# Attention and two feed-forward networks: weights converted in pairs in place, casts on ScalarE, split products with v from the second batch on

## The chip, the cores and the metric

The kernel runs on one core of one Trainium2 chip. The metric is the device time of one execution in microseconds (us); of several executions the median counts. The profile is of one execution, and its durations and waits are read from the hardware's own records.

## The reference

Three parts follow one another; all inputs and the output are float32.

```python
def _attn_ref(q, k, v, f):            # q, k, v: (4, 8, 576, 64), f: (4, 8, 576)
    scores = scale * np.matmul(q, k.transpose(0, 1, 3, 2))
    log_f = np.log(np.clip(f, 0.0001, 1.0))
    cum = np.cumsum(log_f, axis=-1)
    decay = cum[:, :, :, None] - cum[:, :, None, :]
    scores = np.where(causal, -1000000000.0, scores + decay)
    attn = np.exp(scores - np.max(scores, axis=-1, keepdims=True))
    attn = attn / (np.sum(attn, axis=-1, keepdims=True) + 1e-09)
    return np.matmul(attn, v).astype(np.float32)

def _moe_ref(x, w_gate, w_val, w_out):   # x: (2304, 512), d_ff 1536; these weights are
    g = x @ w_gate                       # float64
    silu = g * (1.0 / (1.0 + np.exp(-g)))
    return (silu * (x @ w_val) @ w_out).astype(np.float32)

def _moe2_ref(x, w_gate, w1, w2):        # 8 experts, inner width 1024
    P = balance(x @ w_gate)              # exp, then 8 rounds of row and column scaling
    return sum(P[:, e:e + 1] * (np.maximum(x @ w1[e], 0.0) @ w2[e]) for e in range(8))
```

(The last function's body is put in short words.) The weights of the first network arrive as 64-bit words, which the kernel turns into float32 itself.

## The kernel before

**Precision.** TensorE multiplies in a fast format of float32 (float32r in the code). To keep float32's accuracy, an operand is split in two float32r values, a high part (a cast, `hi`) and the rest (`rest`, line 153: source minus high part, on GpSimd unless told otherwise). A product is then the sum of three fast products (`three`, line 157), or of two where one operand is treated so. Products with plain float32 operands are also possible on TensorE; each shows as two matmul records.

**Attention** (`attn_unit`, line 233) works batch by batch, head by head, two heads to a pair. `load` (257) fetches q and k of a head twice, into both halves of the partitions, and the row of decays; line 277 casts q and k to float32r on VectorE, and two `rest` calls on GpSimd make their low parts. `scores` (286) multiplies a block of 128 queries with the keys, adds the decay and takes the minimum on VectorE (line 304), and the exponential on ScalarE (line 308). `trans` (331) transposes the probabilities on TensorE and copies them from PSUM. `pv` (351) multiplies them with v in two ranges of queries. `recips` (312) adds 1e-9 to the sums of a pair of heads (line 315, VectorE), takes the reciprocal, transposes it, and sends it through DRAM to be broadcast; `fold` (376) multiplies it in.

In the first two batches (`first`, `b < FRONT`, FRONT = 2) the products with v are plain float32: `trans` copies (line 343, on VectorE for blocks 2 and 4, on ScalarE for the others), into one set of buffers for each head of a pair; `pv` makes one product a block and one copy (365). In the last two batches the products are split: v is cast on ScalarE (250, 253) and its rest made on GpSimd (252, 254), with both parts side by side in one stationary operand; `trans` casts (347, ScalarE) and subtracts (348, VectorE) into one set of buffers, `pv` makes two products a block, and line 373 copies and 374 adds the two halves. `spaces` (205) allocates these buffers. Batches 0 and 1 also take their PSUM for scores from the pool of the first network, which does not run yet.

**The first network** (`moe_unit`, line 415) goes through d_ff in six slices of 256. A slice needs six pieces of weights: gate and value for each of two blocks of 128 columns, and two output pieces. `convert` (107) makes a piece from float64: a load of 512 KB to `st` (four issues for gate and value, one for an output piece), on VectorE the exponent's bits (123), on ScalarE their shift (125), on VectorE sign and exponent (126), the exponent alone (128) and the mantissa's product (129), on GpSimd a sum (131), then the high part (134, ScalarE) and the rest (135, GpSimd; its time is under line 155). The result goes to a ring of eight buffers (`wring`) and is also stored in DRAM (`wsplit`, 136). Each of the 36 pieces is converted once, during batches 0 and 1 of this network; batches 2 and 3 fetch the stored pieces (`fetch`, 148).

**The second network** starts behind it and is most of the time: lines 605 to 672, with weights prefetched.

**Order.** `merge` (21) interleaves steps of attention and of the network by their costs: batch 0 alone, batch 1 with the first six conversions, batch 2 with the network on batches 0 and 1 (converting on the way), batch 3 with the network on batch 2, then the network on batch 3 with the preparation of the second network (510 to 558). The compiler's scheduler then orders each engine's queue by its own model of times, so loads can be issued far ahead of their place in the program; each engine works its queue in order. All transfers are issued by SP. The loads of the first PACE (4) pieces are held behind the last load of q and k issued before them.

Of the kernel before, what the change touches and what calls it, by code (L numbers as in the profile page):

```python
# [8 lines left out]
F32 = mybir.dt.float32  # L9
F32R = mybir.dt.float32r  # L10
# [23 lines left out]
def attention_two_ffns(ctx: ExitStack, tc: tile.TileContext, qkT, vt, f, w_gate, w_val, w_out, g2, w1, w2, out):  # L34
# [3 lines left out]
    DFF = w_gate.shape[1]  # L38
# [16 lines left out]
    wring = m_ctx.enter_context(pool("wring", 8))  # L55
# [36 lines left out]
    bases = const.tile([P, 2], F32, name="bases")  # L92
    nc.vector.memset(bases[:, 0:1], -8.0 * (896 << 4))
    nc.vector.memset(bases[:, 1:2], -8.0 * (897 << 4))
    wpieces = []
    for s in range(nsl):
        for c in range(2):
            f0 = s * FS + c * P
            for w in (w_gate, w_val):
                wpieces.append((w[:, f0:f0 + P].rearrange("(k p) f -> p k f", p=P), KD, bases[:, 0:1]))  # L100
        for c in range(2):
            f0 = s * FS + c * P

            wpieces.append((w_out[f0:f0 + P, :], 1, bases[:, 1:2]))
    wsplit = [dram.tile([P, 2, HP], F32, name=f"wsplit{i}") for i in range(len(wpieces))]

    def convert(i):
        src, nk, base = wpieces[i]
        st = cvp.tile([P, 4 * HP + 4], U16, tag="st", name="st", bufs=2)
        n = HP // nk  # L110
        with tc.issue_after(last_qk[0].ins) if i < PACE else ExitStack():
            if nk == 1:
                nc.sync.dma_start(out=st[:, 1:1 + 4 * HP], in_=src.bitcast(U16))
            else:
                for k in range(nk):
                    nc.sync.dma_start(out=st[:, 1 + 4 * n * k:1 + 4 * n * (k + 1)], in_=src[:, k, :].bitcast(U16))
        mid = st.bitcast(U32)[:, 0:2 * HP].rearrange("p (i t) -> p i t", t=2)[:, :, 1]
        top = st[:, 4:4 + 4 * HP].rearrange("p (i t) -> p i t", t=4)[:, :, 0]
        y = cvp.tile([P, HP], U16, tag="y", name="y")
        z = cvp.tile([P, HP], U16, tag="z", name="z")  # L120
        g = cvp.tile([P, HP], U16, tag="g", name="g")
        v = cvp.tile([P, HP], F32, tag="v", name="v")
        nc.vector.tensor_scalar(out=y, in0=top, scalar1=0x7fff, scalar2=None, op0=ALU.bitwise_and)

        nc.scalar.activation(out=z, in_=y, func=AF.Relu, scale=8.0, bias=base)
        nc.vector.scalar_tensor_tensor(
            out=g, in0=top, scalar=0x8000, in1=z, op0=ALU.bitwise_and, op1=ALU.bitwise_or)
# [3 lines left out]
        nc.gpsimd.tensor_tensor(out=v, in0=v, in1=g.bitcast(BF16), op=ALU.add)  # L131
        t = wring.tile([P, 2, HP], F32R, tag="w", name="w")
        hi, lo = t[:, 0], t[:, 1]
        nc.scalar.copy(out=hi, in_=v)
        rest(lo, v, hi)
# [6 lines left out]
    PACE = 4  # L142

    FRONT = 2
    VIA = 2
    ONV = (2, 4)

    def fetch(i):
        t = wring.tile([P, 2, HP], F32R, tag="w", name="w")
        last_dma[0] = nc.sync.dma_start(out=t.bitcast(F32), in_=wsplit[i])  # L150
        return t
# [53 lines left out]
    def spaces(b):  # L205


        first = b < FRONT
# [24 lines left out]
    def attn_unit(b):  # L233
        first = b < FRONT
        pairs, heads = {}, {}

        def load_pair(hp):
            if hp == 0:
                if b != VIA:
                    room(b)  # L240
                if b in (0, FRONT):
                    spaces(b)
# [14 lines left out]
        def load(h):  # L257
# [19 lines left out]
            nc.vector.tensor_copy(out=qkh, in_=qk)  # L277
# [8 lines left out]
        def scores(h, qi):  # L286
# [9 lines left out]
            for n, (c0, w, use) in enumerate(chunks):  # L296
                ps = (ps_m if first else ps_s).tile([P, 512], F32, tag="m" if first else "s", name="ps_s")
# [14 lines left out]
        def recips(hp):  # L312

            rc = small.tile([P, 10], F32, tag="rc", name="rc", bufs=2)
            nc.vector.tensor_scalar_add(out=rc, in0=sms[hp % 2], scalar1=1e-9)
# [15 lines left out]
        def trans(h, qi):  # L331
            pt = heads[h][-1].pop(qi)
            alt = first and qi % 3 == 2
# [78 lines left out]
    def group(w):  # L412
        return [w[0], w[2]], [w[1], w[3]], w[4:6]
# [348 lines left out]
```

## Time and profile before

| What | Value |
|---|---|
| Median of three runs | 2308.84 us |
| Lowest and highest | 2297.91 and 2312.47 us |
| The profiled execution | 2307.45 us |
| Its span, first to last instruction | 2305.7 us |
| Mean granted TensorE clock | 0.990 of full speed |
| TensorE matmul busy | 2246.2 us (97%) |
| TensorE weight loads busy | 2037.2 us (88%) |
| VectorE busy | 1724.4 us (75%) |
| GpSimd busy | 867.1 us (38%) |
| ScalarE busy | 809.5 us (35%) |

The engines are named PE (TensorE; PEld its weight loads), DVE (VectorE), ACT (ScalarE), POOL (GpSimd) and SP (SyncE, which issues the transfers; SPq is its sequencer). Busy times of matmuls overlap their waits, so weight loads tell better how full TensorE is. A row of a group gives line, engine, operation, output and inputs, shapes and count, then busy time, mean ns of one, and the idle time before them with what ended it. An execution is 1.75 us longer than its span.

### The profile page before, as it was taken

How to read it: one execution, taken by the hardware profiler on the slowest of the kernel's cores; microseconds unless marked ns; L12 is line 12 of the kernel's file. 1: busy time of each engine (PE TensorE's matmuls, PEld its weight loads, DVE VectorE, ACT ScalarE, POOL GpSimd, SP SyncE). 2: the span in 40 equal slices, each digit the busy share in tenths (PEclk: the TensorE clock that was granted, in tenths of full speed). 3: DMA queues.
4: the chain of work that ended last, by engine and by line, in shares of the span. 5: the costliest groups of instructions: out<-in, count | busy, mean ns of one | idle time of the engine just before them, and what ended most of it. 6: DMA issues, size and time to landing. Idle time of an engine off the chain costs nothing.

```text
span 2305.7 us, 36555 instructions
## 1 busy us (share of the span) xinstructions
PE 2246.2 (97%) x13913; PEld 2037.2 (88%) x13913; DVE 1724.4 (75%) x3460; ACT 809.5 (35%) x1882; POOL 867.1 (38%) x656
## 2 busy tenths in 40 slices
PE   8999989999999999999999999989999999999999
PEld 6679989989999888989899998979899989899887
DVE  6887777753423688878788887896878888787876
ACT  6665455462122433222232322233323222222321
POOL 4676556553132432323232332362323223232320
PEclk9899999999999999999999999999999999999999
DMA  6765545434545110111111111121111111111111
GB/s 166 219 188 158 166 142 171 146 135 168 182 136 194 61 50 34 56 37 56 37 50 43 46 46 37 56 80 56 56 37 46 46 43 50 37 55 38 50 33 51
DMA packets 114560, 199.34 MB, mean 86 GB/s; under 512 B 12040, under 2 KB 66544, under 8 KB 113872
## 3 DMA queue, kind: packets, MB, share of 16 engines
q1 hardware_dynamic: 114384, 197.01, 26.8%
q8 instruction: 109, 1.79, 0.3%
q14 instruction: 67, 0.55, 0.1%
HBM read 167.25 MB, written 29.72 MB: 85 GB/s over the span
## 4 chain that ended last, share of the span: by engine, by line
PE 84%; DVE 7%; DMA 4%; issue 2%; SPq 1%; ACT 1%; POOL 1%; DVEq 0%; POOLq 0%; ACTq 0%
PE py L163 38%; PE pa L617 30%; PE pm L163 10%; PE ps_o L362 1%; PE ps_t L339 1%; DMA xst<-xd 1%; PE ps_s L302 1%; DVE xt L547 1%; PE ps_s L298 1%; PE ps_o L370 1%; DVE al L632 1%; DMA st<-w_out 1%; DVE np L304 1%; DMA st<-w_gate 1%; DMA st<-w_val 1%
## 5 line engine op out<-in xcount | busy, mean ns | idle before, releaser
L617 PE MATMUL pa<-xf,w1h 128*128 128x288 f32 x3584 | 752.5, 297 | 9.8 <-DVE c L626 6.9
L617 PEld LDWEIGHTS pa<-xf,w1h 128*128 128x128 f32 x3584 | 600.5, 189 | 49.2 <-DVE c L626 8.6
L669 DVE SCALAR_TENSOR_TENSOR acc<-py,lg,acc 128x512 f32<-128x512 f32 x531 | 395.3, 745 | 244.5 <-PE py L163 244.3
L617 PE MATMUL pa<-xf,w1l 128*128 128x288 f32 x1792 | 529.4, 296 | 0.0
L155 POOL TENSOR_TENSOR w2l<-w,w2h 128x1024 fp32r<-128x1024 f32 x64 | 154.8, 2420 | 809.5 <-ACT w2h L593 809.4
L163 PE MATMUL py<-w2h,ah 128*128 128x512 f32 x1152 | 454.4, 394 | 1.6 <-DVE acc L669 1.2
L163 PE MATMUL py<-w2l,ah 128*128 128x512 f32 x1152 | 454.5, 395 | 0.0
L163 PE MATMUL py<-w2h,al 128*128 128x512 f32 x1152 | 453.7, 394 | 0.0
L632 DVE SCALAR_TENSOR_TENSOR al<-c,ah 128x288 fp32r<-128x288 f32 x512 | 426.8, 861 | 6.7 <-ACT ah L631 6.2
L631 ACT ACTIVATE ah<-c 128x288 fp32r<-128x288 f32 x512 | 207.9, 443 | 577.9 <-PE py L163 319.2
L617 PEld LDWEIGHTS pa<-xf,w1l 128*128 128x128 f32 x1792 | 338.6, 189 | 10.7
L163 PE MATMUL pm<-xh,w 128*128 128x288 f32 x1536 | 323.6, 298 | 6.9 <-DVE th L447 4.3
L163 PEld LDWEIGHTS pm<-xh,w 128*128 128x128 f32 x1536 | 252.8, 189 | 9.3 <-DVE th L447 5.0
L163 PEld LDWEIGHTS py<-w2h,al 128*128 128x128 f32 x1152 | 216.6, 188 | 49.5
L163 PEld LDWEIGHTS py<-w2h,ah 128*128 128x128 f32 x1152 | 216.9, 188 | 30.1 <-DVE acc L669 2.7
L163 PEld LDWEIGHTS py<-w2l,ah 128*128 128x128 f32 x1152 | 216.7, 188 | 25.9
L155 POOL TENSOR_TENSOR w1l<-w,w1h 128x256 fp32r<-128x256 f32 x192 | 162.1, 871 | 191.2 <-ACT w1h L589 174.8
L163 PE MATMUL pm<-xl,w 128*128 128x288 f32 x768 | 228.0, 297 | 0.0
L637 ACT COPY m<-pa 128x288 f32<-128x288 f32 x128 | 50.3, 393 | 437.7 <-PE pa L617 433.7
L163 PE MATMUL py<-ah,w 128*128 128x288 f32 x768 | 172.4, 300 | 6.6 <-DVE th L447 4.5
L155 POOL TENSOR_TENSOR al<-th,ah 128x288 fp32r<-128x288 f32 x96 | 81.6, 850 | 201.6 <-ACT ah L449 200.7
L155 POOL TENSOR_TENSOR w1l<-sm,w1h 128x1024 fp32r<-128x1024 f32 x64 | 155.1, 2424 | 1.9 <-ACT w1h L589 1.9
(141 smaller groups left out, 3122.4 us busy)
## 6 DMA issues: line engine op xcount, KB each, us to landing
w<-w SPq DMA_DIRECT2D x128, 512.0 KB
w<-wsplit SPq DMA_DIRECT2D x72, 512.0 KB
qk<-qkT SPq DMA_DIRECT2D x64, 288.0 KB
wsplit<-w SPq DMA_DIRECT2D x36, 512.0 KB
cb<-cumd SPq DMA_DIRECT2D x31, 288.0 KB
st<-w_gate SPq DMA_DIRECT2D x48, 128.0 KB
st<-w_val SPq DMA_DIRECT2D x48, 128.0 KB
st<-w_out SPq DMA_DIRECT2D x12, 512.0 KB
```

The lines of the kernel that those rows point to most:

```text
L155: (eng or nc.gpsimd).tensor_tensor(out=out, in0=src, in1=hi.bitcast(F32), op=ALU.subtract)
L163: nc.tensor.matmul(out=ps, lhsT=a, rhs=b, start=(i == 0), stop=(i == n - 1))
L298: nc.tensor.matmul(out=ps[:, 0:w], lhsT=a[:, qs:qs + P], rhs=kh[:, c0:c0 + w], start=True, stop=False)
L302: nc.tensor.matmul(out=ps[:, 0:w], lhsT=a[:, qs:qs + P], rhs=kl[:, c0:c0 + w], start=False, stop=True)
L304: nc.vector.tensor_tensor_reduce(out=pt[r0:P, c0:c0 + use], in0=ps[r0:P, 0:use], in1=cb[r0:P, c0:c0 + use], scale=-SCALE, scalar=prev, op0 ...
L339: nc.tensor.transpose(pv[:, j, :], pt[r0:P, k0:k0 + P], ident[r0:P, r0:P])
L362: nc.tensor.matmul(out=po[:, c0:w], lhsT=vs[r0:P, j, :], rhs=pts[rng][e][r0:P, j, c0:w], start=(i == 0), stop=(i == len(order) - 1))
L617: nc.tensor.matmul(out=ps, lhsT=w[:, MW[m - 1], k], rhs=x[:, m - 1, hl, k], start=(n == 0), stop=(n == len(ops) - 1))
L631: nc.scalar.activation(out=ah[:, f, tk], in_=src, func=AF.Relu)
L632: nc.vector.scalar_tensor_tensor(out=al[:, f, tk], in0=src, scalar=0.0, in1=ah[:, f, tk].bitcast(F32), op0=ALU.max, op1=ALU.subtract)
L637: nc.scalar.copy(out=m1, in_=p1)
L669: nc.vector.scalar_tensor_tensor(out=a, in0=py, scalar=lg[:, t, e:e + 1], in1=a, op0=ALU.mult, op1=ALU.add)
```

## The change

Weights: the host lays the weights of the first network out in 18 pairs (`wf`): gate and value of one block of 128 columns, or the two output pieces of a slice, 1 MB each, 8 KB to a partition. `convert` handles a pair at once, with one load; the float32 result `v` is written over the raw words of `st` (every second 32-bit word), the shifted exponent over `g`, and only the sum, the high part and the rest are done in two halves. `y` and `g` have one buffer, the ring four buffers of twice the size.

Attention: the cast of q and k (line 277) and the 1e-9 (line 315) move from VectorE to ScalarE. The plain float32 products with v are used for batch 0 only (WIDE = 1); batch 1 is split like the last two, while its scores and transposes keep the PSUM pools of the first two batches (`early`). The load hold (PACE) covers two pairs instead of four pieces. A small buffer of `finish` moves to another pool.

```diff
-    wring = m_ctx.enter_context(pool("wring", 8))
+    wring = m_ctx.enter_context(pool("wring", 4))
...
-    wsplit = [dram.tile([P, 2, HP], F32, name=f"wsplit{i}") for i in range(len(wpieces))]
+    nc.vector.memset(bases[:, 2:3], 1e-9)
+    wsplit = [dram.tile([P, 2, 2, HP], F32, name=f"wsplit{i}") for i in range(NPC)]
 
     def convert(i):
-        src, nk, base = wpieces[i]
-        st = cvp.tile([P, 4 * HP + 4], U16, tag="st", name="st", bufs=2)
-        n = HP // nk
+        base = bases[:, 1:2] if i % 3 == 2 else bases[:, 0:1]
+        W = 2 * HP
+        st = cvp.tile([P, 4 * W + 4], U16, tag="st", name="st", bufs=2)
         with tc.issue_after(last_qk[0].ins) if i < PACE else ExitStack():
-            if nk == 1:
-                nc.sync.dma_start(out=st[:, 1:1 + 4 * HP], in_=src.bitcast(U16))
-            else:
-                for k in range(nk):
-                    nc.sync.dma_start(out=st[:, 1 + 4 * n * k:1 + 4 * n * (k + 1)], in_=src[:, k, :].bitcast(U16))
-        mid = st.bitcast(U32)[:, 0:2 * HP].rearrange("p (i t) -> p i t", t=2)[:, :, 1]
-        top = st[:, 4:4 + 4 * HP].rearrange("p (i t) -> p i t", t=4)[:, :, 0]
-        y = cvp.tile([P, HP], U16, tag="y", name="y")
-        z = cvp.tile([P, HP], U16, tag="z", name="z")
-        g = cvp.tile([P, HP], U16, tag="g", name="g")
-        v = cvp.tile([P, HP], F32, tag="v", name="v")
+            nc.sync.dma_start(out=st[:, 1:1 + 4 * W], in_=wf[i].bitcast(U16))
+
+        def words(dt):
+            return st.bitcast(dt)[:, 0:2 * W].rearrange("p (i t) -> p i t", t=2)[:, :, 1]
+        mid, v = words(U32), words(F32)
+        top = st[:, 4:4 + 4 * W].rearrange("p (i t) -> p i t", t=4)[:, :, 0]
+        y = cvp.tile([P, W], U16, tag="y", name="y", bufs=1)
+        g = cvp.tile([P, W], U16, tag="g", name="g", bufs=1)
         nc.vector.tensor_scalar(out=y, in0=top, scalar1=0x7fff, scalar2=None, op0=ALU.bitwise_and)
 
-        nc.scalar.activation(out=z, in_=y, func=AF.Relu, scale=8.0, bias=base)
+        nc.scalar.activation(out=g, in_=y, func=AF.Relu, scale=8.0, bias=base)
         nc.vector.scalar_tensor_tensor(
-            out=g, in0=top, scalar=0x8000, in1=z, op0=ALU.bitwise_and, op1=ALU.bitwise_or)
+            out=g, in0=top, scalar=0x8000, in1=g, op0=ALU.bitwise_and, op1=ALU.bitwise_or)
...
-        nc.gpsimd.tensor_tensor(out=v, in0=v, in1=g.bitcast(BF16), op=ALU.add)
-        t = wring.tile([P, 2, HP], F32R, tag="w", name="w")
-        hi, lo = t[:, 0], t[:, 1]
-        nc.scalar.copy(out=hi, in_=v)
-        rest(lo, v, hi)
+        t = wring.tile([P, 2, 2, HP], F32R, tag="w", name="w")
+        halves = [slice(j * HP, (j + 1) * HP) for j in range(2)]
+        for h in halves:
+            nc.gpsimd.tensor_tensor(out=v[:, h], in0=v[:, h], in1=g[:, h].bitcast(BF16), op=ALU.add)
+        for j, h in enumerate(halves):
+            nc.scalar.copy(out=t[:, j, 0], in_=v[:, h])
+            rest(t[:, j, 1], v[:, h], t[:, j, 0])
         nc.sync.dma_start(out=wsplit[i], in_=t.bitcast(F32))
...
-    PACE = 4
+    PACE = 2
 
     FRONT = 2
+    WIDE = 1
...
     def spaces(b):
-        first = b < FRONT
+        first = b < WIDE
...
     def attn_unit(b):
-        first = b < FRONT
+        first, early = b < WIDE, b < FRONT
...
-                if b in (0, FRONT):
+                if b in (0, WIDE):
                     spaces(b)
...
-            nc.vector.tensor_copy(out=qkh, in_=qk)
+            nc.scalar.copy(out=qkh, in_=qk)
...
-                ps = (ps_m if first else ps_s).tile([P, 512], F32, tag="m" if first else "s", name="ps_s")
+                ps = (ps_m if early else ps_s).tile([P, 512], F32, tag="m" if early else "s", name="ps_s")
...
-            nc.vector.tensor_scalar_add(out=rc, in0=sms[hp % 2], scalar1=1e-9)
+            nc.scalar.activation(out=rc, in_=sms[hp % 2], func=AF.Identity, bias=bases[:, 2:3])
...
-            alt = first and qi % 3 == 2
+            alt = early and qi % 3 == 2
...
-        return [w[0], w[2]], [w[1], w[3]], w[4:6]
+        return [w[0][:, 0], w[1][:, 0]], [w[0][:, 1], w[1][:, 1]], [w[2][:, 0], w[2][:, 1]]
...
-                w = [get(6 * s + i) for i in range(6)]
+                w = [get(3 * s + i) for i in range(3)]
...
-                ls = frm.tile([P, HB], F32, tag="ls", name="ls", bufs=1)
+                ls = tmp.tile([P, HB], F32, tag="th", name="ls")
...
-    merge(attn_unit(1), [(1.0, lambda i=i: w0.append(convert(i))) for i in range(6)])
+    merge(attn_unit(1), [(1.0, lambda i=i: w0.append(convert(i))) for i in range(3)])
```

## Rows read from the trace of the kernel before

**Rows 1.** Windows: stretch, length, busy PE, PEld, DVE, ACT, POOL; clock, DMA share, GB/s
```profile
0.00:54.00 54.00, 45.02 (x260) 34.76 (x260) 35.05 (x114) 32.62 (x90) 23.98 (x25) 1.00 0.65 162
54.00:144.00 90.00, 82.35 (x437) 61.40 (x437) 76.32 (x188) 62.16 (x165) 66.44 (x46) 0.89 0.79 226
144.00:350.00 206.00, 191.36 (x1380) 180.16 (x1380) 155.12 (x361) 108.94 (x273) 119.85 (x105) 0.98 0.49 155
350.00:520.00 170.00, 165.03 (x1222) 157.01 (x1221) 116.67 (x296) 92.20 (x225) 97.30 (x85) 0.99 0.45 147
520.00:770.00 250.00, 241.04 (x1775) 238.37 (x1775) 97.44 (x203) 60.10 (x134) 73.46 (x70) 0.99 0.47 160
```

**Rows 2.** Chain of waits from 54 to 144 us, shares by line
```profile
by line: PE ps_o L362 16.1%; issue 9.6%; DMA st<-w_gate 9.0%; PE ps_t L339 7.6%; DVE np L304 7.2%; PE ps_s L298 6.2%; DVE g L126 5.6%; PE ps_s L302 5.4%; SPq L116 5.0%; DMA st<-w_val 4.5%; DVE y L128 3.1%; DVE y L123 2.7%; DVE qkh L277 2.6%
```

**Rows 3.** VectorE's groups by line and shape, 0 to 520 us
```profile
L129 DVE SCALAR_TENSOR_TENSOR v<-st,y 128x512 f32<-128x512 uint32 x36 | 36.7, 1020 | 4.9 <-POOL w L155 4.7
L126 DVE SCALAR_TENSOR_TENSOR g<-st,z 128x512 uint16<-128x512 uint16 x36 | 29.8, 830 | 4.1 <-ACT z L125 2.5 <-POOL al L155 0.9 <-POOL kl L155 0.6
L277 DVE CAST qkh<-qk 128x1152 fp32r<-128x1152 f32 x32 | 27.5, 858 | 6.0 <-DMA qk<-qkT 5.3
L123 DVE TENSOR_SCALAR y<-st 128x512 uint16<-128x512 uint16 x36 | 27.4, 762 | 15.0 <-DMA st<-w_gate 7.2 <-DMA st<-w_out 4.4 <-DMA st<-w_val 3.1
L128 DVE TENSOR_SCALAR y<-g 128x512 uint16<-128x512 uint16 x36 | 17.9, 497 | 0.3
L315 DVE TENSOR_SCALAR rc<-sm 128x10 f32<-128x10 f32 x16 | 13.9, 870 | 3.8 <-ACT np L308 3.8
```

**Rows 4.** Single lines: ns shortest/median/longest, first and last start in us
```profile
L123 DVE TENSOR_SCALAR y<-st x36: 406/582/1429, 60.3 to 412.9; 128x512 uint16<-128x512 uint16 x36
L128 DVE TENSOR_SCALAR y<-g x36: 276/294/1362, 65.2 to 416.4; 128x512 uint16<-128x512 uint16 x36
L315 DVE TENSOR_SCALAR rc<-sm x16: 173/938/1394, 25.0 to 495.2; 128x10 f32<-128x10 f32 x16
```

**Rows 5.** GpSimd's groups, 0 to 520 us
```profile
L155 POOL TENSOR_TENSOR kl<-qk,qkh 128x576 fp32r<-128x576 f32 x32 | 48.1, 1502 | 2.5
```

**Rows 6.** ScalarE's groups: line 551 after 770 us, the others 0 to 520 us
```profile
L551 ACT CAST xf<-xt 128x1152 fp32r<-128x1152 f32 x4 | 4.6, 1158 | 8.9 <-DVE xt L547 8.9
...
L347 ACT CAST pt<-ps_t 128x128 fp32r<-128x128 f32 (+4 forms) x80 | 32.7, 424 | 13.1 <-PE ps_t L339 12.2
L343 ACT COPY pt<-ps_t 128x128 f32<-128x128 f32 (+2 forms) x48 | 19.1, 405 | 4.3 <-PE ps_t L339 3.7
...
L250 ACT CAST vs<-vr 128x512 fp32r<-128x512 f32 x8 | 5.0, 621 | 0.2
```

**Rows 7.** VectorE's groups of the products with v, 0 to 520 us
```profile
L348 DVE TENSOR_TENSOR pt<-ps_t,pt 128x128 fp32r<-128x128 f32 (+4 forms) x80 | 38.2, 484 | 7.1 <-ACT pt L347 6.4
L343 DVE COPY pt<-ps_t 128x384 f32<-128x384 f32 (+1 forms) x32 | 16.6, 519 | 0.6 <-PE ps_t L339 0.2
...
L374 DVE TENSOR_TENSOR bt<-ps_o,bt 64x320 f32<-64x320 f32 x16 | 7.8, 486 | 9.4 <-ACT bt L373 9.2
L374 DVE TENSOR_TENSOR bt<-ps_o,bt 64x256 f32<-64x256 f32 x16 | 6.7, 418 | 3.2 <-ACT bt L373 2.9
```

**Rows 8.** GpSimd's split of V, 0 to 520 us
```profile
L155 POOL TENSOR_TENSOR vs<-vr,vs 128x256 fp32r<-128x256 f32 x16 | 12.2, 781 | 4.7 <-issue 2.5 <-ACT vs L250 1.4 <-POOL vs L155 0.8
```

**Rows 9.** Pieces of the chain in order of time: start us, us, what
```profile
155.09 2.50 PE ps_o L362 x10
...
352.26 1.36 PE ps_o L370 x10
```

**Rows 10.** SP's waits from 50 to 450 us: us in total, times, longest
```profile
SPq L136 <- POOL w L155: 30.1, 16, 9.1
```

**Rows 11.** Windows around the first fall of the clock, columns as in rows 1
```profile
54.00:60.70 6.70, 5.13 (x28) 3.43 (x28) 1.48 (x6) 3.68 (x10) 5.33 (x4) 1.00 0.79 214
60.70:71.00 10.30, 9.77 (x32) 7.40 (x33) 7.43 (x20) 5.78 (x16) 4.33 (x4) 0.50 0.65 175
```

More of the change, by code (lines that the diff above doesn't have):

```diff
@@ L33, in attention_two_ffns @@
 @with_exitstack
-def attention_two_ffns(ctx: ExitStack, tc: tile.TileContext, qkT, vt, f, w_gate, w_val, w_out, g2, w1, w2, out):
+def attention_two_ffns(ctx: ExitStack, tc: tile.TileContext, qkT, vt, f, wf, g2, w1, w2, out):
     nc = tc.nc
@@ L37, in attention_two_ffns @@
     NT, DM = out.shape
-    DFF = w_gate.shape[1]
+    NPC = wf.shape[0]
+    DFF = NPC * 256 // 3
     E, _, F2 = w1.shape
@@ L91, in attention_two_ffns @@
     nsl = DFF // FS
-    bases = const.tile([P, 2], F32, name="bases")
+    bases = const.tile([P, 3], F32, name="bases")
     nc.vector.memset(bases[:, 0:1], -8.0 * (896 << 4))
     nc.vector.memset(bases[:, 1:2], -8.0 * (897 << 4))
[L95 to L104, printed above, removed]
@@ L148, in fetch @@
     def fetch(i):
-        t = wring.tile([P, 2, HP], F32R, tag="w", name="w")
+        t = wring.tile([P, 2, 2, HP], F32R, tag="w", name="w")
         last_dma[0] = nc.sync.dma_start(out=t.bitcast(F32), in_=wsplit[i])
@@ L743 @@
     B, H, S, D = q.shape
+    wg, wv, wo = (np.ascontiguousarray(inputs[n]) for n in ("moe_w_gate", "moe_w_val", "moe_w_out"))
+    F = wg.shape[1]
+    up = np.stack([wg, wv]).reshape(2, -1, 128, F // 256, 2, 128).transpose(3, 4, 2, 0, 1, 5).reshape(F // 256, 2, 128, -1)
+    dn = wo.reshape(F // 256, 2, 128, -1).transpose(0, 2, 1, 3).reshape(F // 256, 1, 128, -1)
+    wf = np.ascontiguousarray(np.concatenate([up, dn], axis=1).reshape(F // 256 * 3, 128, -1))
     arrays = {
@@ L747 @@
         "f": np.ascontiguousarray(inputs["f"]),
-        "w_gate": np.ascontiguousarray(inputs["moe_w_gate"]).view(np.int64),
-        "w_val": np.ascontiguousarray(inputs["moe_w_val"]).view(np.int64),
-        "w_out": np.ascontiguousarray(inputs["moe_w_out"]).view(np.int64),
+        "wf": wf.view(np.int64),
         "g2": np.ascontiguousarray(inputs["moe2_w_gate"]),
```

## The prediction

> **What bounds the kernel now.** I read the busy time by stage first. Four stages matter: batch 0 (to 54 us), batch 1 with the first weight conversions (54 to 144), batches 2 and 3 beside the first network (144 to 520), and what follows. The stage after 520 shows TensorE at its limit: weight loads fill 238 of 250 us, and the second network behind it (TensorE busy for 97% of the whole span) is not touched by the change. So the answer lies in the first 520 us [rows 1]. There the weight loads fill 35 of 54, 61 of 90 and 337 of 376 us, while VectorE is busy 35, 76 and 272 us. From 54 to 144 VectorE, at 85%, is the fullest engine; the others stand at 69% (ScalarE), 74% (GpSimd) and 79% (the DMA engines).
>
> Next the chain of waits of that stage. It runs through all engines: matmuls about a third, then VectorE's conversion lines (126, 128, 123), the landing of weight pieces (9.0 + 4.5%) and the issuing of these transfers on SP (5.0%) [rows 2]. A conversion step sits in VectorE's queue in front of the scores' reduction, so a late piece stops attention as well.
>
> Then VectorE's groups [rows 3]. A conversion of one piece costs 762 + 830 + 497 + 1020 ns = 3.11 us, 36 times 112 us; the cast of q and k 858 ns, 32 times; and line 315, which handles ten columns, 870 ns. That last is no work: the shortest of them took 173 ns and the median 938. Line 128 shows the same, 276 to 1362 ns [rows 4]. The stretched ones are as long as one GpSimd subtraction, 1.5 us [rows 5]: they stand behind GpSimd.
>
> The Trainium skill (SBUF — State Buffer, "Who interferes with whom") says that VectorE's copies, casts and scalar operations in a two-port mode and GpSimd shut each other out for a whole instruction, and that ScalarE never waits. The stretched line 315 agrees.
>
> **The change, part by part.**
>
> *The casts move to ScalarE.* VectorE loses 16 x 0.858 = 13.7 us in the first two batches and as much in the last two. ScalarE gains the same count at 1.158 us, the duration of its cast of exactly 128x1152 in the later stage [rows 6]: 18.5 us in either half.
>
> *Line 315 moves too.* VectorE loses 8 x 0.87 = 7.0 us in either half. ScalarE's price for ten columns is not shown; it lies between nothing and 0.4 us (its copies of 128 to 512 columns [rows 6]); I take 0.3, so 2.4 us. I expect no activation-table load: in this kernel lines 125, 446 and 343 (Relu, Tanh, copies) alternate with line 308's Exp already.
>
> *Pairs of pieces.* The columns stay, half the instructions go. The fixed part of a VectorE instruction follows from line 374: 418 ns for 256 columns, 486 for 320, so 1.06 ns a column and 0.147 us fixed [rows 7]. Free of waiting, a piece costs 0.41 (shortest of line 123) + 0.69 + 0.28 + 0.69 (512 x 1.06 + 147) = 2.07 us, and a pair 4.14 - 4 x 0.147 = 3.55. The waiting on top is 3.11 - 2.07 = 1.04 us a piece. It lies between unchanged (it goes with the time on the port) and halved (it goes with the instructions). A stretched instruction waits for one GpSimd instruction, whatever its own length [rows 4, 5]; I take half. Eight pieces (what the ring holds) fall in the first two batches: 24.9 us become 4 x 3.55 + 4.2 = 18.4, saving 6.5. The other 28: 87.1 become 49.7 + 14.6 = 64.3, saving 22.8 (8.3 at the other end).
>
> By the skill's exclusive lock of the same section the wait is set by the GpSimd instruction in front, so half goes; if waiting went with time on the port, none of it would.
>
> On GpSimd the count stays (two halves). Its sums now read words 8 bytes apart; the nearest row, a split of V in short runs, is 781 ns for 256 columns against 1502 for 576 [rows 5, 8], 17% more per column. Bounds are none and 17% of some 100 us; it has room (66 of 90 us busy), so I cost it at nothing. Where GpSimd became late, the store of the split weights on SP would be late next, and every load queued behind it.
>
> The loads: four issues for a gate or value piece (one for an output piece) become one a pair, of 1 MB. In batch 1 SP's issuing of them was 5.0% of the chain, 4.5 us, and the landings 13.5%, 12 us [rows 2]. The new landing is bounded by one old one (4 us) and two (8); I let half as many landings cost as much in total, and take 2 us off for the issues.
>
> *Batch 1 with split V and probabilities.* TensorE saves: the long product of a head took 2.50 us, the split one 1.36 [rows 9]. About 9 us go, but TensorE was not the bound there, so I count nothing. VectorE per head: five subtractions of 484 ns for two copies of 519, and two sums of 418 and 486 ns [rows 7]: 2.42 - 1.04 + 0.90 = 2.28 us, eight times 18.3. ScalarE: five casts of 424 for three copies of 405, 0.9 us a head, 7.2 us; and the casts of V, 0.62 us and a smaller one a pair of heads [rows 6], together 3.7. GpSimd gets two subtractions of 0.78 and a smaller one a pair of heads [rows 8], about 8 us.
>
> *The sum.* First two batches, VectorE: 111.4 - 13.7 - 7.0 - 6.5 + 18.3 = 102.5 us. ScalarE: 32.6 + 62.2 + 18.5 + 2.4 + 7.2 + 3.7 = 126.6 us of 144, of which some 9 at the start are spent waiting for the first scores. ScalarE becomes the fullest engine. At VectorE's present fullness (85%) the two batches take 126.6/0.85 + 9 = 158 us, 14 more; at 95%, 142, or 2 fewer. I take 90%: 149.7, so +6, less the 2 of the issues: **+4 us**. Batches 2 and 3: VectorE falls from 272 to 272 - 13.7 - 7.0 - 22.8 = 228 of 376 us; ScalarE, 201 + 21, stays under 60%. If TensorE ran there as in the stage after 520 (95% weight loads), 337 us of loads would need 354, so 23 us are to be had [rows 1]. VectorE's waits for landings (15 us in all, line 123 [rows 3]) stay about half. I take half: **-12 us**. After 520 the ring is fetched in 1 MB steps, half as many, under matmuls that fill 95%; nothing. Together -8 us: 2307.45 of the profiled execution becomes 2299.5. The median shown is 1.4 above that execution, so **2301 us**, against 2308.8.
>
> **Rivals.**
>
> *All of the relief comes back* (faster). VectorE's waits are what opens the gaps in TensorE, and all 23 us go; in batches 0 and 1 GpSimd and VectorE stop shutting each other out and ScalarE packs at 95%, -4 with the issues. For it: 272 us of VectorE fall by 16%. Against it: 376 us with 90% weight loads leave little. -27: 2282.
>
> *ScalarE and the clock turn batches 0 and 1 into the loss* (slower). Split products need a further step (ScalarE's cast, VectorE's subtraction, then the product), with one set of buffers instead of one for each head of a pair. At 80% fullness 126.6/0.8 + 9 = 167, or +23; decided by whether ScalarE stands idle at over a fifth of the stage. TensorE's shorter work helps this on: after the stall from 54 to 60.7 us the granted clock was 0.50 (1.2 GHz) for 10 us [rows 11], and with 9 us less work between the same waits such stretches last longer. With -5 in the later stage: 2327.
>
> The skill (TensorE: Matmul & The Clock Gate, Part 1) says that the slow clock is the resting state and work lifts it; rows 11 agree, and by that rule batch 1 alone would lose.
>
> *The stage buffer holds too long* (slower). Today the buffer of a raw piece is free after line 129; in place, it is free only after GpSimd's last subtraction, which waits for a ring slot. The next load waits for that at the head of SP's queue, with the loads of q, k and the sums behind it. SP already waits 30 us for that subtraction [rows 10]. If each of 14 pairs came 4 us late on VectorE and half of that reached TensorE, +28 stand against the -12 and +4: 2329. It decides once a load starts less than its landing, some 5 us, before line 123's turn. Against it: 14 pairs are spread over some 270 us (line 123 runs until 413 us [rows 4]).
>
> **How the numbers follow.** Forecast 0.58, full relief 0.23, ScalarE and clock 0.11, stage buffer 0.08. The forecast's own range is 2288 to 2314 (the later stage -20 to -5, the first two batches -2 to +14, less overlap of the ends). With the rivals, the range is 2270 to 2327. One per cent, 23 us, is about what a measurement of this kernel can tell. Full relief passes it most of the time and the forecast seldom, so faster 0.26; the two slower rivals pass it in some two thirds of their cases, slower 0.13; within, 0.61.
>
> **What would show it.** Right: ScalarE at 88% or more from 54 to the end of batch 1, VectorE at some 75% there; line 277 near 1.16 us on ScalarE; conversion instructions at 18 each, line 123 near 0.7 us when not stretched, with fewer stretched; weight loads above 91% in batches 2 and 3; no change in the second network's length. Wrong: batch 1 ending well before 140 us, long waits of VectorE for landings, ScalarE sitting behind VectorE's subtractions, new table loads, or a longer stage after 520.

## The result, and the profile after

The changed kernel takes 2318.58 us (median of 9 runs), the kernel before beside it 2305.23: a ratio of **1.0065, 95% interval 1.0046 to 1.0084**, 13 us slower. The time lies within the range that was forecast and on the other side of no change from the forecast.

The stages of the changed kernel (windows; columns as in rows 1), with one further stretch at the end of the first network:

```profile
0.00:54.00 54.00, 43.91 (x239) 33.57 (x240) 27.28 (x106) 41.23 (x102) 26.50 (x26) 0.97 0.65 158
54.00:144.00 90.00, 72.03 (x402) 54.36 (x400) 72.12 (x178) 72.95 (x175) 71.40 (x54) 0.89 0.79 235
144.00:350.00 206.00, 200.88 (x1497) 191.77 (x1498) 143.07 (x336) 128.12 (x312) 130.27 (x112) 0.99 0.49 157
350.00:520.00 170.00, 157.32 (x1153) 148.98 (x1153) 106.05 (x258) 94.07 (x217) 97.80 (x81) 0.98 0.44 147
520.00:770.00 250.00, 241.96 (x1770) 239.11 (x1769) 96.22 (x199) 60.09 (x134) 69.45 (x67) 0.98 0.45 155
...
768.00:785.00 17.00, 7.45 (x33) 5.47 (x33) 1.37 (x4) 5.79 (x11) 10.48 (x8) 0.69 0.28 102
```

Against rows 1: up to 144 us VectorE falls and ScalarE rises, as worked out, and from 54 to 144 VectorE, ScalarE and GpSimd stand at 79 to 81%; in batches 2 and 3 the weight loads fill 341 of 376 us instead of 337. None of that is a loss of 13 us. The last line is: for 17 us behind the first network's last product TensorE's weight loads fill 5.5 us, and the granted clock falls to 0.69.

When the first network's gate and value products ("gate products" from here on) ran, in both kernels (the line of TensorE's products `pm`: count, ns shortest/median/longest, first and last start in us), before:

```profile
L163 PE MATMUL pm<-xh,w x1536: 287/295/443, 147.1 to 761.1; 128*128 128x288 f32 x192
```

and after:

```profile
L156 PE MATMUL pm<-xh,w x1536: 288/295/608, 151.5 to 761.7; 128*128 128x288 f32 x192
```

So the first network begins 4.4 us later and ends only 0.6 us later. Half-way (the 769th of these products) the trace has 512.8 before and 509.2 after: batches 2 and 3 brought 8 us, and 4 us of that were lost again by 761. The rest is lost in the few microseconds that follow. TensorE's queue there, in order of time (start us, us, engine, line, operation; in brackets the idle time and what ended it), of the changed kernel:

```profile
769.98 0.40 PE L474 MATMUL pl<-f,gh 128*128 128x288 f32 x1 [0.80 <-ACT f L470]
771.46 0.40 PE L474 MATMUL pl<-f,gh 128*128 128x288 f32 x1 [1.08 <-POOL f L148]
...
778.78 0.61 PE L474 MATMUL pl<-f,gh 128*128 128x288 f32 x1 [0.88 <-POOL f L148]
...
780.82 0.59 PE L677 MATMUL pz<-ident,ls 8*128 8x8 f32 x4 [0.48 <-ACT ls L478]
784.80 0.56 PE L677 MATMUL pz<-ident,ls 8*128 8x8 f32 x4 [3.39 <-DMA ls<-lgd]
785.29 0.85 PE L610 MATMUL pa<-xf,w1h 128*128 128x288 f32 x2
```

`finish` makes the logits of the last batch (`pl`), each product waiting for a cast and a subtraction; then the second network's gate transposes (`pz`) wait for logits that must come back from DRAM; and only then come the second network's own products (`pa`, line 610; 30 of them were made earlier, from 636 to 699 us). TensorE is left with few and widely spaced products for 16 us. The chain of waits tells the same (start us, us, what):

```profile
781.75 2.91 DMA ls<-lgd
784.66 0.14 issue
784.80 0.56 PE pz L677 x4
785.36 4.62 PE pa L610 x18
```

In the kernel before, TensorE is full there:

```profile
761.00:778.00 17.00, 16.36 (x123) 16.12 (x122) 12.73 (x30) 7.03 (x15) 5.13 (x4) 1.00 0.17 71
```

Its queue has second-network products between those of the logits. What was changed at this place is one line, the small buffer `ls` for the logits on their way to DRAM.

The conversion after, and the moved operations (groups, 0 to 520 us):

```profile
L119 DVE SCALAR_TENSOR_TENSOR st<-st,y 128x1024 f32<-128x1024 uint32 x18 | 29.7, 1648 | 0.2
L116 DVE SCALAR_TENSOR_TENSOR g<-st,g 128x1024 uint16<-128x1024 uint16 x18 | 27.8, 1544 | 5.2 <-ACT g L115 5.0
L113 DVE TENSOR_SCALAR y<-st 128x1024 uint16<-128x1024 uint16 x18 | 16.8, 934 | 14.7 <-DMA st<-wf 14.6
...
L118 DVE TENSOR_SCALAR y<-g 128x1024 uint16<-128x1024 uint16 x18 | 16.3, 904 | 0.3
...
L270 ACT CAST qkh<-qk 128x1152 fp32r<-128x1152 f32 x32 | 36.9, 1154 | 15.3 <-DMA qk<-qkT 8.1 <-PE ps_s L295 7.2
...
L308 ACT ACTIVATE rc<-sm,bases 128x10 f32<-128x10 f32 x16 | 4.8, 299 | 0.2
...
L124 POOL TENSOR_TENSOR st<-st,g 128x512 f32<-128x512 f32 x36 | 43.9, 1241 | 12.0 <-DVE st L119 7.1 <-issue 3.6 <-ACT pt L336 1.2
```

Conversion on VectorE went from 112 to 90.6 us [rows 3]. The cast takes 1.154 us on ScalarE (1.158 was taken), line 315's successor 0.30 (0.3), and GpSimd's sums over words 8 bytes apart 1.241 us, no more than the 1.266 before.

### The profile page after: what moved, and what is told of

Same layout as the page of the kernel before. It is cut to its first block, busy times and chain, and to the rows that moved or that the text cites. A ratio compares the mean times of both kernels' runs of the same rounds, so it can differ in the third digit from the quotient of the medians.

```text
span 2316.8 us, 36241 instructions
## 1 busy us (share of the span) xinstructions
PE 2242.6 (97%) x13913; PEld 2036.5 (88%) x13913; DVE 1686.1 (73%) x3381; ACT 851.3 (37%) x1936; POOL 879.2 (38%) x668
## 4 chain that ended last, share of the span: by engine, by line
PE 64%; DVE 1%; issue 0%; POOL 0%; DMA 0%; ACT 0%; SPq 0%; DVEq 0%; POOLq 0%
PE py L156 34%; PE pa L610 30%; DVE al L625 1%; DVE xt L540 0%; DVE acc L662 0%; DVE c L619 0%; DMA ls<-lgd 0%; POOL f L148 0%; POOL w1l L148 0%; PE pz L677 0%; DVE u L619 0%; ACT xf L544 0%; PE pz L704 0%; ACT ah L624 0%; SPq L568 0%
## 5 line engine op out<-in xcount | busy, mean ns | idle before, releaser
L625 DVE SCALAR_TENSOR_TENSOR al<-c,ah 128x288 fp32r<-128x288 f32 x512 | 418.9, 845 | 14.2 <-ACT ah L624 12.9
```

The costliest lines, as they stand in the source:

```text
L625: nc.vector.scalar_tensor_tensor(out=al[:, f, tk], in0=src, scalar=0.0, in1=ah[:, f, tk].bitcast(F32), op0=ALU.max, op1=ALU.subtract)
```

## The experiments

**e1 and e2: the buffer `ls`.** In the changed kernel `ls` lies in the two buffers of `th`, the tanh of the network. e1 undoes that line alone; e2 makes it alone in the kernel before.

```diff
# e1, against the changed kernel
-                ls = tmp.tile([P, HB], F32, tag="th", name="ls")
+                ls = frm.tile([P, HB], F32, tag="ls", name="ls", bufs=1)
# e2, against the kernel before: the same line the other way round
```

> The changed kernel with one edit undone: the small buffer ls of finish is again a buffer of its own in the pool frm; nothing else differs. Theory A (that buffer is the loss: shared with th it makes the tanh of the next slice, and at the end the second network's first temporaries, wait for the logits' transfer): the time falls from 2318.6 to 2297 to 2306 us, ratio to the kernel before 0.996 to 1.001; TensorE's hole between the last logits products and the second network's first full products (some 12 us at 768 to 785 us) closes, and the first output product starts near 783 us instead of 799. Theory B (ScalarE, fuller in the first two batches, is the loss): the time stays at 2315 to 2320, ratio 1.005.

> The kernel before with that one edit made: ls of finish in th's buffers, nothing else. Theory A: 11 to 19 us slower than the kernel before, 2316 to 2324 us, ratio 1.005 to 1.008, with the hole at the start of the second network. Theory B: no change, 2305 us, ratio 0.999 to 1.001.

e1: 2299.45 us, ratio to the kernel before 0.9971 (0.9960 to 0.9982). e2: 2325.2 us, ratio 1.0084 (1.0069 to 1.0098). One line is worth 19 us either way (2318.58 against 2299.45, and 2325.2 against 2305.99 of the kernel before beside it); theory B fell. TensorE's queue in e1 at the same place:

```profile
761.45 0.29 PE L474 MATMUL pl<-f,gl 128*128 128x288 f32 x1
761.58 0.45 PE L610 MATMUL pa<-xf,w1h 128*128 128x288 f32 x2
761.87 0.29 PE L610 MATMUL pa<-xf,w1l 128*128 128x288 f32 x1
...
764.00 0.29 PE L474 MATMUL pl<-f,gh 128*128 128x288 f32 x1
764.12 0.42 PE L610 MATMUL pa<-xf,w1h 128*128 128x288 f32 x2
```

The second network's products (610) fill the waits of the logits' (474). The same 17 us as a window, in e1:

```profile
754.00:771.00 17.00, 16.54 (x125) 16.30 (x123) 12.64 (x30) 6.86 (x15) 5.13 (x4) 1.00 0.17 71
```

and in e2, where the hole is back:

```profile
780.00:797.00 17.00, 7.84 (x34) 5.73 (x33) 1.41 (x4) 5.79 (x11) 10.09 (x8) 0.67 0.28 103
```

**e10: shared, or in the wrong place?** `ls` stays in the pool `tmp`, in a buffer of its own. When the first network's pools are closed, the second network's temporaries are laid where they were, and `tmp` is opened before `frm`, so it would stand nearer their start (read from the code; addresses are in no trace).

```diff
# against the changed kernel
-                ls = tmp.tile([P, HB], F32, tag="th", name="ls")
+                ls = tmp.tile([P, HB], F32, tag="ls", name="ls", bufs=1)
```

> The changed kernel with ls in the pool tmp as there, but in a buffer of its own instead of th's. Theory S (sharing th's two buffers is the loss, at every finish and at the last): 2297 to 2303 us, as e1. Theory P (at the end it is the place: the second network's first temporaries lie where tmp lay, and wait until ls has been sent): the hole at the start of the second network stays, the first output product starts 12 us or more after the last gate product's 20 us mark of e1, and the total is 2307 to 2314.

2311.27 us, ratio 1.0018 (1.0006 to 1.0029): both are at work. The holes behind the two earlier `finish` steps, in the changed kernel at 515 to 522 us and at 650 to 653, are gone (around the first of these steps TensorE is idle for 2.7 us instead of 7.0), so sharing with `th` cost some 7 us (2318.6 to 2311.3). The one at the end is still there, and costs the other 12 (2311.3 to 2299.5):

```profile
765.71 0.61 PE L474 MATMUL pl<-f,gh 128*128 128x288 f32 x1 [0.80 <-ACT f L470]
...
768.70 0.59 PE L677 MATMUL pz<-ident,ls 8*128 8x8 f32 x4
773.26 0.56 PE L677 MATMUL pz<-ident,ls 8*128 8x8 f32 x4 [3.97 <-DMA ls<-lgd]
773.75 0.85 PE L610 MATMUL pa<-xf,w1h 128*128 128x288 f32 x2
```

From the last gate product to ScalarE's first copy of an output (line 653) it takes 37.0 us in the changed kernel and 36.9 in e10, but 26.4 in e1 and 25.2 before. ScalarE's queue shows what the place does. The second network's first temporary, `m`, copied from its first product, came ahead of the last logits in the kernel before:

```profile
767.87 0.40 ACT L637 COPY m<-pa 128x288 f32<-128x288 f32 x1 [3.69 <-PE py L163]
...
781.18 0.38 ACT L485 COPY ls<-pl 8x288 f32<-8x288 f32 x1
```

In e1 they stand so too (761.04 and 774.35). In the changed kernel `m` comes directly behind them:

```profile
780.38 0.39 ACT L478 COPY ls<-pl 8x288 f32<-8x288 f32 x1 [0.33 <-PE pl L474]
780.68 0.38 ACT L630 COPY m<-pa 128x288 f32<-128x288 f32 x1
```

In e10 it does so as well (768.80 and 769.10).

**e3: the cast alone.**

```diff
# against the kernel before
-            nc.vector.tensor_copy(out=qkh, in_=qk)
+            nc.scalar.copy(out=qkh, in_=qk)
```

> The kernel before with only the cast of q and k moved to ScalarE. Theory 1 (VectorE is what holds attention up and ScalarE has room): 3 to 8 us faster, ratio 0.9965 to 0.9987, batch 0 some 3 us shorter, batches 2 and 3 a few us. Theory 2 (ScalarE becomes the fullest engine in the first two batches): those two batches 4 us or more longer, the total 0 to 6 us slower.

2305.63 us, ratio 1.0001 (0.9989 to 1.0012). Neither theory: 27 us of work taken from VectorE bring nothing in all.

**e4: plain products in batch 1 too.**

```diff
# against e1
-    WIDE = 1
+    WIDE = 2
```

> The changed kernel with ls back in a buffer of its own and plain float32 products with v for batch 1 as well (WIDE 2). Theory 1 (the split of v and of the probabilities is what makes batch 1 longer, by 8 us from its first to its last exponential): 4 to 10 us faster than with ls back alone, batch 1's exponentials within 72 to 76 us. Theory 2 (the conversion in pairs makes it longer): no change against ls back alone, batch 1 stays at 80 us or more.

2284.82 us, ratio 0.9912 (0.9898 to 0.9926): 14.6 us faster than e1, more than theory 1 gave, with batch 1 shorter than it gave too. Batch 1's exponentials (the 41st to the 80th of all) take 73.7 us before, 82.0 after, 83.1 in e1 and 69.4 in e4. The gate products start at 138.7 us instead of e1's 153.0, so the whole gain is there by the end of batch 1.

**e5 and e6: what the pairs bring.** e5 is e4 with the cast back on VectorE; e6 has line 315's successor back as well, and is the kernel before with nothing but the pairs.

```diff
# e5, against e4
-            nc.scalar.copy(out=qkh, in_=qk)
+            nc.vector.tensor_copy(out=qkh, in_=qk)
# e6, against e5
-            nc.scalar.activation(out=rc, in_=sms[hp % 2], func=AF.Identity, bias=bases[:, 2:3])
+            nc.vector.tensor_scalar_add(out=rc, in0=sms[hp % 2], scalar1=1e-9)
```

> As e4 (ls in a buffer of its own, plain float32 products with v in batches 0 and 1), and the cast of q and k back on VectorE: of the change only the pairs and the 1e-9 on ScalarE are left. Theory 1 (the pairs bring the gain by themselves; the cast is worth nothing, as e3 showed beside single pieces): 2282 to 2289 us, within 3 us of e4's 2284.8. Theory 2 (beside the pairs the cast counts, since VectorE is emptier and the port freer): 2291 to 2300 us.

> The kernel before with the pairs alone (the 1e-9 back on VectorE too). Theory 1 (line 315's time on VectorE is waiting for GpSimd that would be spent anyway): within 2 us of e5. Theory 2 (its 14 us on VectorE lie in the way of attention): 4 to 10 us slower than e5. The conversion instructions: 18 each; if waiting goes with the number of instructions, about half of the single pieces' waiting of 38 us is left, if it goes with the time on the port, all of it.

e5: 2294.86 us, ratio 0.9955 (0.9940 to 0.9970). e6: 2286.22 us, ratio 0.9922 (0.9908 to 0.9937). The pairs alone are 18 us faster than the kernel before; the two moves to ScalarE together add nothing (e4, 1.4 us less), and line 315 moved without the cast loses 8.6 us: e5 alone would speak for the cast (theory 2), and that e6 is faster than e5 neither of e6's theories had. The cause stays open. The queues are ordered anew for each kernel, which may bring such a difference, but that was not shown. Differences of a few microseconds between these kernels are not read here, and the prices of single parts below are no surer than that. The gain of the pairs lies in the first network. Its gate products in e1 and in e6:

```profile
L156 PE MATMUL pm<-xh,w x1536: 288/295/445, 153.0 to 754.3; 128*128 128x288 f32 x192
L156 PE MATMUL pm<-xh,w x1536: 288/295/537, 146.4 to 741.5; 128*128 128x288 f32 x192
```

From the first to the last they take 614.0 us before, 601.3 in e1 and 595.1 in e6. VectorE's conversion groups in e6:

```profile
L116 DVE SCALAR_TENSOR_TENSOR g<-st,g 128x1024 uint16<-128x1024 uint16 x18 | 26.6, 1481 | 3.9 <-ACT g L115 3.9
...
L119 DVE SCALAR_TENSOR_TENSOR st<-st,y 128x1024 f32<-128x1024 uint32 x18 | 25.7, 1430 | 0.1
...
L113 DVE TENSOR_SCALAR y<-st 128x1024 uint16<-128x1024 uint16 x18 | 16.8, 934 | 19.0 <-DMA st<-wf 18.9
L118 DVE TENSOR_SCALAR y<-g 128x1024 uint16<-128x1024 uint16 x18 | 15.9, 883 | 0.2
```

85 us instead of 112; 4 us of the difference come back in the cast of q and k (31.7 us in e6 instead of 27.5). VectorE waits for landings 18.9 us, no less than before (15.0 [rows 3]): the larger transfers did not shorten that.

**e7, e8, e9, e12, e13, e14: why the split makes batch 1 longer.** Each changes one thing that only the split batch has. Against e1:

```diff
# e7: PSUM of the transposes spread over both pairs of buffers
-            alt = early and qi % 3 == 2
+            alt = early and (qi % 2 == 0 if not first else qi % 3 == 2)
# e8: no low part of the probabilities in batch 1
-            nc.vector.tensor_tensor(
-                out=lo[:, 0:n, c:c + w], in0=pv, in1=hi[:, 0:n, c:c + w].bitcast(F32), op=ALU.subtract)
+            if b != 1:
+                nc.vector.tensor_tensor(
+                    out=lo[:, 0:n, c:c + w], in0=pv, in1=hi[:, 0:n, c:c + w].bitcast(F32), op=ALU.subtract)
-            ops = [(j, part) for j in order for part in range(2)]
+            ops = [(j, part) for j in order for part in range(1 if b == 1 else 2)]
# e9: the low part of v in batch 1 on VectorE
-                    rest(vs[:, 0:4, h, 1, :], v4[:, 0:4, h], vs[:, 0:4, h, 0, :])
+                    rest(vs[:, 0:4, h, 1, :], v4[:, 0:4, h], vs[:, 0:4, h, 0, :], nc.vector if b == 1 else None)
...
-                rest(vs[64:128, 4, :, 1, :], v4[64:128, 4], vs[64:128, 4, :, 0, :])
+                rest(vs[64:128, 4, :, 1, :], v4[64:128, 4], vs[64:128, 4, :, 0, :], nc.vector if b == 1 else None)
# e12: every product of batch 1 with v made twice
+            for _ in range(2 if b == 1 else 1):
                 for i, (j, part) in enumerate(ops):
# e13: as e8, and a set of buffers for each head of a pair
+            if b == 1:
+                hi = pts[qi // 2 > 0][h % 2]
...
-                    out=po[:, c0:w], lhsT=vs[:, j, e].rearrange("p a d -> p (a d)"), rhs=pts[rng][part][:, j, c0:w],
+                    out=po[:, c0:w], lhsT=vs[:, j, e].rearrange("p a d -> p (a d)"), rhs=pts[rng][e if b == 1 else part][:, j, c0:w],
```

e14, against e4, goes the other way (plain products, one set of buffers); e11 gives e4 the PSUM of e7:

```diff
# e14
-                copy(out=pts[qi // 2 > 0][h % 2][:, 0:n, c:c + w], in_=pv)
+                copy(out=pts[qi // 2 > 0][0 if b == 1 else h % 2][:, 0:n, c:c + w], in_=pv)
...
-                        out=po[:, c0:w], lhsT=vs[r0:P, j, :], rhs=pts[rng][e][r0:P, j, c0:w],
+                        out=po[:, c0:w], lhsT=vs[r0:P, j, :], rhs=pts[rng][0 if b == 1 else e][r0:P, j, c0:w],
# e11
-            alt = early and qi % 3 == 2
+            alt = early and qi % 2 == 0
```

> As e1 (ls in a buffer of its own, batch 1 split), but batch 1's transposes use the second pair of PSUM buffers for blocks 0, 2 and 4 instead of block 2 alone. Theory P (split transposes hold their two PSUM buffers through a cast and a subtraction, and TensorE waits for them): batch 1's exponentials shrink from 83 to 72 to 78 us and the total falls by 5 to 12 us to 2288 to 2295. Theory W (the added work on ScalarE and VectorE is what counts, wherever it stands): 2297 to 2301 us, as e1.

> As e1, but in batch 1 the low part of the probabilities is left out: neither the subtraction on VectorE nor the second product of each block (the split of v and the sum of the two halves stay). It leaves out part of the computation. Theory V (the subtractions behind the casts, five a head, make batch 1 longer): batch 1's exponentials take 70 to 75 us, as with plain products, and the total falls to 2284 to 2290 us. Theory S (ScalarE, which gains casts of q, k, v and of the probabilities, makes it longer): 80 us or more, the total 2295 to 2300 us.

> As e1 (ls in a buffer of its own, batch 1 split), but the low parts of v of batch 1 are made on VectorE instead of GpSimd (three subtractions a pair of heads). Theory G (GpSimd, busy 97% from 72 to 122 us in e1, is what makes batch 1 longer): batch 1's exponentials shrink from 83 to 73 to 78 us, the total to 2287 to 2294. Theory D (the added steps of the split products count, whichever engine has them): 80 us or more and 2296 to 2303 us in all.

> As e1 (ls in a buffer of its own, batch 1 split), but TensorE makes every product with v of batch 1 twice (the second overwrites the first; the result is the same), about 1.8 us more a head, nearly what the plain products took. Theory C (with less work TensorE falls to 1.2 GHz between the waits, in e1 for a seventh of the time from 54 to 155 us in excess of e4, and this is what makes batch 1 longer): the clock there rises from 0.86 to 0.93 or more, batch 1's exponentials shrink from 83 to 74 to 79 us, the total falls to 2289 to 2296. Theory W (the other engines' added steps are the cause): batch 1 stays at 82 us or grows, the total is 2298 to 2312.

> As e8 (ls in a buffer of its own; batch 1 with split v, the low part of the probabilities left out), but batch 1's odd heads put their high parts into the buffers that the low parts would have had, so each head of a pair has a set of its own, as with the plain products. It leaves out part of the computation. Theory B (one set of buffers ties each head's transposes to the products of the head before): batch 1's exponentials shrink from 81 to 70 to 75 us and the total from 2295 to 2284 to 2290. Theory W (the casts, splits and sums added to the chain): 79 us or more, 2291 to 2297.

> As e4 (ls in a buffer of its own, plain products in batches 0 and 1), but batch 1's heads share one set of buffers for the transposed probabilities instead of one for each head of a pair. Theory B: batch 1's exponentials grow from 69 to 76 us or more, the total from 2285 to 2291 to 2299. Theory W: 68 to 72 us, 2283 to 2288.

> As e4 (ls in a buffer of its own, plain products in batches 0 and 1), with the transposes of blocks 0, 2 and 4 of both batches in the second pair of PSUM buffers, as in e7 for batch 1. If e7's gain came from PSUM buffers held too long: 2277 to 2282 us. If plain copies free them early enough: 2283 to 2287.

| Kernel | Time, us | Ratio to before (95%) | Batch 1's exponentials, us | First gate product, us | Clock, 54 to 155 us |
|---|---|---|---|---|---|
| e1 | 2299.45 | 0.9971 (0.9960 to 0.9982) | 83.1 | 153.0 | 0.86 |
| e7, PSUM spread | 2289.58 | 0.9938 (0.9922 to 0.9954) | 82.1 | 146.0 | 0.90 |
| e8, no low part | 2295.22 | 0.9957 (0.9941 to 0.9972) | 80.9 | 145.9 | 0.88 |
| e9, v's low part on VectorE | 2304.96 | 0.9998 (0.9988 to 1.0007) | 90.0 | 161.4 | 0.83 |
| e12, products twice | 2304.00 | 0.9991 (0.9976 to 1.0005) | 91.9 | 159.4 | 0.93 |
| e13, no low part, two sets | 2283.24 | 0.9894 (0.9880 to 0.9909) | 78.4 | 145.9 | 0.85 |
| e4, plain products | 2284.82 | 0.9912 (0.9898 to 0.9926) | 69.4 | 138.7 | 0.97 |
| e14, plain, one set | 2280.98 | 0.9887 (0.9868 to 0.9906) | 68.7 | 138.3 | 1.00 |
| e11, plain, PSUM spread | 2286.86 | 0.9914 (0.9901 to 0.9927) | 65.7 | 131.0 | 0.93 |

The last three columns are of one execution each (e8's is its fastest, 2290.16 us). By the exponentials none of the suspects is it by itself. Without the subtractions, without the PSUM limit, or with buffers for each head the batch stays at 78 us or more, and one set of buffers costs the plain batch nothing. What e13 keeps of the split is v's own cast and low part, the products made from them, the sum of the two halves, and two more copies of the probabilities a head on ScalarE; it still needs 9 us more than e4.

The total time tells something else. Spreading the PSUM brings the split batch 10 us (e1 to e7) and the plain one nothing (e4 to e11), so the price of the split falls from 0.6% (e1 against e4) to 0.2% (e7 against e11, which spreads batch 0's transposes too). Of e7's 10 us, 7 are there at the first gate product, though batch 1's exponentials are only 1 us shorter. So e7 met theory P in the total and theory W in the exponentials; the PSUM is the strongest suspect that is left, and how it works was not shown. e13's first gate product comes when e8's does, so its 12 us lie later and say nothing on this.

The clock is no likely cause: it was not lower in the changed kernel (0.90 from 54 to 155 us) than in the kernel before (0.88) whose batch was 8 us shorter, and in e12 more work for TensorE held it up (0.93) and the batch was longer all the same. e12 alone does not rule it out, since the doubled products take time themselves. GpSimd, which was busy for 48.8 of the 50 us from 72 to 122 in e1, was emptier in e9 (40.4), and with its work on VectorE the batch was 7 us longer. The engines in that stage (windows), e1:

```profile
54.00:155.00 101.00, 82.92 (x455) 63.87 (x454) 77.93 (x200) 82.15 (x198) 84.20 (x61) 0.86 0.76 225
```

e9:

```profile
54.00:155.00 101.00, 80.66 (x415) 60.28 (x413) 81.17 (x199) 77.17 (x185) 69.42 (x48) 0.83 0.74 219
```

and e4:

```profile
54.00:155.00 101.00, 92.60 (x551) 70.94 (x549) 74.77 (x183) 80.09 (x196) 76.84 (x57) 0.97 0.82 232
```

In e1 VectorE, ScalarE and GpSimd all stand at 77 to 83% while each head goes through all three in turn; in e4, with TensorE doing more and the others somewhat less, it goes faster. That would fit a batch held up by the length of its chain rather than by one engine, but it was not shown. What is shown is the price of the split in the changed kernel, 14.6 us (e1 against e4).

The best of these kernels that compute everything are e14, e4, e11 and e6, at 0.9887 to 0.9922 of the kernel before: pairs in place, plain products in both first batches, `ls` as it was.

## Why the prediction was right or wrong

**The first two batches, +4: right in sum, wrong in its parts.** The first gate product came 4.4 us later, but that the sum came out is luck. It was put on ScalarE as the fullest engine in both batches. Batch 0, where this was expected too, became 3.5 us shorter (its last exponential at 71.5 us instead of 75.0), and batch 1 8.3 longer (82.0 for 73.7). ScalarE's own sum was well sized (123.8 us up to 155, for 126.6), its place was not: from 54 to 144 it was busy for 81%, not 88 or more, level with GpSimd and with VectorE, which was to fall to 75%. "TensorE was not the bound there, so I count nothing" stands: its shorter products did not help. The working added the split up engine by engine, and no single engine was found that paid for it: the price shown is 14.6 us of time (e1 against e4). Without the split the first gate product came 8.4 us earlier than before (e4).

**The pairs: right in mechanism, the gain under-sized.** A pair free of waiting takes 0.68 + 1.22 + 0.41 + 1.21 = 3.52 us by the shortest of the four lines (3.55 was worked out). A single piece takes 1.97 us by the same measure (2.07 was worked out, with 0.69 for line 129, whose shortest took 0.62), so the waiting on top was 41 us before, not 37. It was taken to halve; 90.6 - 18 x 3.52 = 27 us were left in the changed kernel, two thirds, and 23 in e6, little over half. VectorE saved 21 us (27 in e6) where 29 were forecast; yet the pairs alone brought 18 us of time (e6), more than the whole later stage was given.

**The cast and line 315: their durations right, their worth wrong.** 1.154 and 0.30 us on ScalarE, and no table load beside the two at the start that the kernel before has as well. But the cast's 27 us less for VectorE were counted, one half in the first two batches and the other towards the -12 us, and e3 shows nothing for it.

**Batches 2 and 3, -12.** From the first to the 769th gate product the changed kernel gained 8 us, within what was bounded (-20 to -5); the weight loads filled 90.6% there, short of the 91 that was to show it. In e1, without the holes of `ls`, the stretch from the first to the last gate product is 12.7 us shorter than before.

**After 520: "nothing". This step failed, and with it the sign.** It looked at the fetches of the ring, and those cost nothing that shows (weight loads 239.1 us of 250 from 520 to 770, for 238.4). It left out an edit that stands in the diff: the buffer `ls`. Nothing was bounded for it, no cover was named. It cost 19 us: without it (e1) the changed kernel stands at 2299.45, where the forecast had 2301, and at 0.9971 of the kernel before. A buffer lent to a second use, or laid where another's will be, takes a place in that one's order as well: the tanh of the next slice came directly behind `ls` (at 522.05 and 521.76 us), and so did the second network's `m` behind the last `ls`. In the kernel before the second network's products covered the logits' small steps; with `ls` in `tmp` that covering work came only behind them. The traces show these orders, and e1, e2 and e10 show that the one line sets them. That it does so through the shared memory is the reading that fits; no trace shows it.

**The rivals.** That ScalarE and the clock make the first two batches a loss: batch 1 alone did lose, but the place is not ScalarE alone, which was idle 19% of the stage like VectorE and GpSimd, and the clock was no lower than before. The stage buffer that is held too long: SP's wait for GpSimd's last subtraction rose from 30 [rows 10] to 49 us, and the pairs gained even so, so it does not decide. Full relief (-27 us, 23 of them in batches 2 and 3): the kernels with plain products and `ls` as it was come nearest, with -21 (e4) and -18 (e6); from the first to the last gate product e6 gained 18.9.

## What to carry to other kernels

Cost every line of a diff, the buffers above all: ask of each one who else holds it, until which transfer, and what is laid on its memory when its pool is closed. When a large change moves the time little, compare when the same instructions start in both traces; the loss then stands in one place, here 16 us long, far from the engines that the change was about. Taking work from a busy engine need not move the time: the cast took 27 us from VectorE and brought nothing (e3), the pairs took as much (112 to 85 us), with one issue of a load where there were eight or two, and brought 18 (e6). Measure a stage by more than one mark: by its exponentials alone the PSUM of e7 looked like nothing, by the first gate product and the total it did not.

## What was not expected of the hardware

What VectorE's conversion instructions take above the shortest of their line did not go with their number: 41 us at 36 pieces, 27 us at 18 pairs (23 in e6). The Trainium skill's exclusive lock (SBUF — State Buffer, "Who interferes with whom") would give one GpSimd instruction as the most that one instruction waits. The trace agrees: in the changed kernel the longest of each of the four lines is 0.9 to 1.1 us above the shortest, and GpSimd's sums and subtractions for the weights took 1.24 and 1.44 us on average. A pair's four instructions were 27/72 = 0.38 us above the shortest on average (0.32 in e6) against 41/144 = 0.28 before. That would fit longer instructions that meet GpSimd more often, which was not shown; the lock alone does not give the half that was taken.

A TensorE kept at work did keep its clock (0.93 instead of 0.86 in e12, where every product of batch 1 with v was made twice), and the batch's exponentials took 9 us longer all the same: a higher granted clock was no gain by itself. (The expectation of e12 puts e1's excess of time at 1.2 GHz over e4 at a seventh; means of 0.86 and 0.97 over the two levels give 28 and 6% of the 101 us, so over a fifth.)
